# wo of kv head 0 by eight 8-partition transfers, two more wo parts in mid-stream, last product and result in two rows: one decode block on one core

## Chip, cores and metric

One core of one Trainium2 chip. The metric is the device time of the whole program in microseconds, lower is better. Within one set of rounds the executions of the kernel before spread over 0.4 to 0.9 us, so most runs were timed in five rounds, in turn with the kernel before on the same chip. The sets ran on different chips: e1 to e4 on chip 10, e5 to e8 and e13 to e18 on chip 6, e9 to e12 on chip 14. For e13 to e16, eleven of the twelve executions of the kernel before are those of e5 to e8.

## The reference, cut to what matters

One token goes through an adaLN-conditioned block: attention over a cache of 32,768 positions with 32 query heads on 8 kv heads, its output projection `wo`, and a ReLU feed-forward part.

```python
h = _layernorm(x) * (1 + ca) + sa
q = (h @ wq)                                  # 32 heads of 128
scores = einsum(q, k) * Dh ** -0.5            # k_cache: (1, 8, 32768, 128) bf16, 67 MB
o = einsum(softmax(scores), v)                # v_cache: the same size
x = x + ga * (o.reshape(1, 1, 4096) @ wo)     # wo: (4096, 512) bf16, 4.2 MB
h = _layernorm(x) * (1 + cb) + sb
x = x + gb * (relu(h @ w1) @ w2)              # w1: (512, 1792), w2: (1792, 512)
return x                                      # (1, 1, 512) bf16
```

Nearly all of it is reading 149.4 MB once.

## The kernel before

All large loads go out from one queue (SP) in a fixed order, `stream`, into a ring of four slots of 32 KB per partition. A load can go out when the tile four places ahead of it in the stream has been consumed. A K or V tile is 4 MB and fills a slot; a wo part takes a whole slot too, however small.

```python
WOP = [(0, Hkv // 2), (Hkv // 2, Hkv // 4), (3 * Hkv // 4, Hkv // 4)]   # wo parts: heads 0-3, 4-5, 6-7
ring = ctx.enter_context(tc.tile_pool(name="ring", bufs=4))
...
stream = [("wm",), ("wq",)] + [("k", 0, (2 * G, 2 * G + 1)) for G in range(NG)]
for g in range(LAST):
    for G in range(NG):
        stream += [(kind, gg, (2 * G, 2 * G + 1)) for kind, gg in (("k", g + 1), ("v", g))]
stream += [("v", LAST, (0, 1)), ("v", LAST, (2,)), ("wo", 0), ("wo", 1), ("v", LAST, (3,)), ("wo", 2)]
stream += [("w1",)] + [("w2", i) for i in range(len(W2P))]
...
# the tail: x1 in four rows (partitions 0, 32, 64, 96), then for each w2 part
for i in range(KT):                                   # KT = 4
    nc.tensor.matmul(
        ffn_ps[32 * i:32 * i + 1, :], lhsT=hidT[:, ft:ft + 1],
        rhs=w2_sb[:, a, b, i * P:(i + 1) * P], start=False, stop=(ft == FT - 1), ...)
...
nc.vector.tensor_tensor(out=o_rows[:], in0=ffn_ps, in1=gb_rows[:], op=ALU.mult)
nc.vector.tensor_tensor(out=o_bf[:], in0=o_rows[:], in1=x1_rows[:], op=ALU.add)
nc.scalar.dma_start(out=out[0, 0].rearrange("(i n) -> i n", i=KT), in_=o_bf[...][:, 0, :])   # 4 rows of 256 B
```

## Time and profile before

| | before |
|---|---|
| median of all runs of the first comparison | 357.46 us (357.26 to 357.66, 4 runs) |
| span of the profiled run | 355.8 us |
| bytes read | 149.43 MB, 432 GB/s over the middle 300 us |
| last V part consumed from | 340.22 us |
| first product with w2 from | 349.56 us |
| last DVE operation ends, span ends | 353.06 us, 355.8 us |

The share of busy time says little here: the DMA share is full from the first slice to the last, so the table follows the tail.

### The profile page before, as it was taken

Reading aid. Unit: us, or ns where it says so; the run is one execution under the profiler, and the core shown is the slowest. Engines: PE = TensorE matmul, PEld = TensorE weight load, DVE = VectorE, ACT = ScalarE, POOL = GpSimd, SP = SyncE. Lnnn points to the kernel's source line nnn. Section 1 sums busy time; section 2 is a strip of 40 time slices with the busy share of each in tenths; the row PEclk is TensorE's granted clock in tenths of the full one; section 3 lists DMA queues with packets and bytes.
Section 4 is the critical chain, followed back from the end, with each engine's and each line's share of the span. In section 5 each row is a group of like instructions: output and inputs, shape, how many; then the busy total and the mean of one; then the engine's idle time right before and its main releaser. Section 6 shows DMA issues by size and latency. Waiting matters only on the chain.

```text
span 355.8 us, 4200 instructions
## 1 busy us (share of the span) xinstructions
PE 274.2 (77%) x1859; PEld 129.9 (37%) x1859; DVE 188.0 (53%) x210; ACT 30.8 (9%) x74; POOL 8.5 (2%) x14
## 2 busy tenths in 40 slices
PE   0552875998689885998499849987799859987754
PEld 0540322343333342443244324433243324335753
DVE  8414696783297409661759157642937184832020
ACT  1022002201200120001100120012000110003000
POOL 9000000000000000000000000000000000000000
PEclk9999968799969996999699978998599969997555
DMA  8999999999999999999999999999999999999993
GB/s 321 442 422 440 431 427 442 429 425 438 435 426 438 431 422 446 427 431 440 424 442 435 422 443 427 431 437 427 431 437 428 427 438 433 424 437 424 408 411 130
DMA packets 6604, 149.69 MB, mean 421 GB/s; under 512 B 697, under 2 KB 698, under 8 KB 1594
## 3 DMA queue, kind: packets, MB, share of 16 engines
q1 hardware_dynamic: 6578, 149.43, 97.9%
q8 instruction: 14, 0.23, 0.2%
q14 instruction: 4, 0.03, 0.0%
q10 hardware_dynamic: 8, 0.00, 0.0%
HBM read 149.42 MB, written 0.00 MB: 420 GB/s over the span
## 4 chain that ended last, share of the span: by engine, by line
DMA 47%; PE 34%; DVE 14%; issue 3%; ACT 0%; SPq 0%; DVEq 0%
DMA Ksb<-in_A_k_cache_dram 42%; PE S_ps L343 18%; PE o_ps L412 12%; DVE KTt L334 11%; DMA Vsb<-in_A_v_cache_dram 3%; DMA w_sb<-in_B_w_dram 2%; PE oT_ps L402 1%; DVE PT_g L381 1%; PE oT_ps L429 1%; DVE S_g L349 1%; PE L_ps L386 0%; SPq L118 0%; PE attnT_ps L461 0%; PE mT_ps L359 0%; ACT X L426 0%
## 5 line engine op out<-in xcount | busy, mean ns | idle before, releaser
L343 PE MATMUL S_ps<-KTt,qbd 128*128 128x512 bf16 x512 | 134.5, 423 | 29.8 <-DVE KTt L334 29.7
L334 DVE STREAM_TRANSPOSE KTt<-Ksb 128x2048 f32<-128x2048 f32 x64 | 142.6, 2279 | 21.1 <-DMA Ksb<-in_A_k_cache_dram 17.0
L412 PE MATMUL o_ps<-Vsb,PT_g 128*16 128x512 bf16 x448 | 99.0, 379 | 0.0
L343 PEld LDWEIGHTS <-qbd 128*128 128x128 bf16 x512 | 53.8, 106 | 104.6 <-issue 53.8
L412 PEld LDWEIGHTS <-PT_g 128*16 128x16 bf16 x448 | 39.1, 90 | 56.8 <-issue 3.0
L436 DVE TENSOR_TENSOR oT_sb<-oT_ps,Linv 128x4 bf16<-128x4 f32 x8 | 1.3, 162 | 71.8 <-PE oT_ps L429 57.3
L349 DVE TENSOR_SCALAR_CACHE_REDUCE S_g<-S_ps 128x512 f32<-128x512 f32 x16 | 11.1, 691 | 41.3 <-PE S_ps L343 41.3
L314 ACT COPY qbd<-qrep_sb 32x128 bf16<-32x128 bf16 x32 | 9.4, 295 | 160.0 <-PE S_ps L343 158.9
L386 PE MATMUL L_ps<-Lexp,ones_f 128*128 128x4 f32 x16 | 3.9, 314 | 13.0 <-DVE Lexp L384 13.0
L426 ACT COPY X<-o_ps 16x512 f32<-16x512 f32 x7 | 4.0, 574 | 110.4 <-PE o_ps L412 110.4
L402 PE MATMUL oT_ps<-PT_g,Vsb 128*128 128x4 bf16 x256 | 7.3, 166 | 4.4 <-DMA Vsb<-in_A_v_cache_dram 2.8
L381 DVE STREAM_TRANSPOSE PT_g<-P_g 128x1024 bf16<-128x1024 bf16 x8 | 9.9, 1232 | 0.0
L429 PE MATMUL oT_ps<-osel,X 16*128 16x4 f32 x56 | 7.3, 250 | 2.5 <-ACT nbias L373 2.5
L197 PE MATMUL xc_ps<-one,c_bd 8*128 8x1 bf16 x4 | 0.3, 172 | 11.6 <-DVE c_bd L187 11.6
L376 ACT ACTIVATE P_g<-S_g,nbias 128x1024 bf16<-128x1024 f32 x8 | 9.2, 1147 | 0.2
L402 PEld LDWEIGHTS <-Vsb 128*128 128x128 bf16 x256 | 7.2, 105 | 4.5 <-DMA Vsb<-in_A_v_cache_dram 2.9
L359 PE MATMUL mT_ps<-ident_f,m_p 128*1 128x128 f32 x8 | 2.2, 269 | 8.4 <-DVE m_p L357 8.4
L386 PEld LDWEIGHTS L_ps<-Lexp,ones_f 128*128 128x128 f32 x16 | 3.6, 271 | 13.5 <-issue 13.4
L155 DVE COPY sel<-ident_bf 128x128 bf16<-128x128 bf16 x4 | 7.8, 3823 | 0.4 <-POOL ident_bf masks.py:199 0.4
L429 PEld LDWEIGHTS oT_ps<-osel,X 16*128 16x128 f32 x56 | 6.7, 186 | 3.1 <-ACT nbias L373 3.1
L292 PE MATMUL qT_ps<-hT,wq_sb 128*128 128x1 bf16 x128 | 3.6, 165 | 3.2 <-DMA wq_sb<-in_A_wq_dram 3.2
L359 PEld LDWEIGHTS mT_ps<-ident_f,m_p 128*1 128x1 f32 x8 | 0.6, 80 | 12.2 <-issue 9.2
(94 smaller groups left out, 79.4 us busy)
## 6 DMA issues: line engine op xcount, KB each, us to landing
Ksb<-in_A_k_cache_dram SPq DMA_DIRECT2D x16, 4096.0 KB, 29.7
Vsb<-in_A_v_cache_dram SPq DMA_DIRECT2D x15, 4096.0 KB, 25.5
wq_sb<-in_A_wq_dram SPq DMA_DIRECT2D x1, 4096.0 KB, 19.7
Vsb<-in_A_v_cache_dram SPq DMA_DIRECT2D x2, 2048.0 KB, 15.5
wm_sb<-in_w_mod_dram SPq DMA_DIRECT2D x1, 3072.0 KB, 10.2
wo_sb<-in_A_wo_dram SPq DMA_DIRECT2D x1, 2048.0 KB
wo_sb<-in_A_wo_dram SPq DMA_DIRECT2D x2, 1024.0 KB, 10.2
w_sb<-in_B_w_dram SPq DMA_DIRECT2D x1, 1792.0 KB, 10.5
```

The source lines that it names most:

```text
L155: nc.vector.tensor_copy(out=sel[:, hp, :].rearrange("p (a c) -> p a c", a=4), in_=src)
L314: nc.scalar.copy(out=o, in_=i)
L334: nc.vector.transpose(out=KTt[:].bitcast(F32), in_=Ksb[:, 32 * half:32 * half + 32, :].rearrange("p j d -> p (j d)").bitcast(F32),)
L343: nc.tensor.matmul(S_ps[:], lhsT=qbd[g % 2][:, hp, s, :], rhs=KTv[:, 16 * sl:16 * sl + 16, h, :, par], start=(t4 == 0 and sl == 0 and hp = ...
L349: nc.vector.tensor_scalar(out=S_tiles[g][:, G, :], in0=S_ps[:], scalar1=1.0, scalar2=None, op0=ALU.mult, op1=ALU.max, accum_out=m_tiles[g] ...
L376: nc.scalar.activation(out=P_g[:], in_=S_g[:].rearrange("p g f -> p (g f)"), func=ACT.Exp, bias=nbias[:], scale=scale, accum_out=l_g[:],)
L381: nc.vector.transpose(out=PT_g[:], in_=P_g[:])
L386: nc.tensor.matmul(L_ps[:], lhsT=ones_f[:], rhs=Lexp[:], start=True, stop=True)
L402: nc.tensor.matmul(o_tiles[g][:], lhsT=Vsb[:, j, :], rhs=PT_g[:, c0:c0 + REP], start=(u == 0 and j == 0), stop=(u == NTILE - 1 and j == TK ...
L412: nc.tensor.matmul(o_tiles[g][:], lhsT=PT_g[:, c0:c0 + 16], rhs=Vsb.rearrange("p (s j) d -> p s j d", j=16)[:, :, j, :], start=(u == 0 and ...
L426: nc.scalar.copy(out=X[:], in_=oT_ps[:])
L429: nc.tensor.matmul(oT_ps[:], lhsT=X[:, s * Dh:(s + 1) * Dh], rhs=osel[:, s, :], start=(s == 0), stop=(s == 3),)
```

## The change

The intent: take wo out of the tail, load the DMA engines more evenly at its end, and make the last product with fewer and wider matmuls and full 512 B rows of output. Cut to its core:

```diff
-    WOP = [(0, Hkv // 2), (Hkv // 2, Hkv // 4), (3 * Hkv // 4, Hkv // 4)]
+    WOP = [(0, 1, P // 2), (1, 1, P), (2, 2, P), (4, 2, P), (6, 2, P)]     # first head, heads, partitions
+    NROW = 2
+    RW = D // NROW
@@ load
+        if kind == "wo_lo":
+            lo = 32 * (key[1] // 4) + key[1] % 4
+            stream_dma(wo_lo[lo:lo + 29:4], wo_v(0)[lo:lo + 29:4])      # 8 partitions of 8 KB
@@ stream
     for g in range(LAST):
+        if g == Hkv // 2:
+            stream += [("wo", 1), ("wo", 2)]
         for G in range(NG):
-            stream += [(kind, gg, (2 * G, 2 * G + 1)) for kind, gg in (("k", g + 1), ("v", g))]
-    stream += [("v", LAST, (0, 1)), ("v", LAST, (2,)), ("wo", 0), ("wo", 1), ("v", LAST, (3,)), ("wo", 2)]
+            for kind, gg in (("k", g + 1), ("v", g)):
+                stream.append((kind, gg, (2 * G, 2 * G + 1)))
+                if 1 <= g < 3:
+                    stream.append(("wo_lo", 4 * (g - 1) + 2 * G + (kind == "v")))
+    stream += [("v", LAST, (0, 1)), ("v", LAST, (2,)), ("wo", 3), ("v", LAST, (3,)), ("wo", 4)]
@@ main loop
+        if g == Hkv // 2:
+            for i in range(3):
+                project(i)
@@ tail
-                for i in range(KT):
+                for i in range(NROW):
                     nc.tensor.matmul(
                         ffn_ps[32 * i:32 * i + 1, :], lhsT=hidT[:, ft:ft + 1],
-                        rhs=w2_sb[:, a, b, i * P:(i + 1) * P], ...
+                        rhs=w2_sb[:, a, b, i * RW:(i + 1) * RW], ...
-    nc.scalar.dma_start(out=out[0, 0].rearrange("(i n) -> i n", i=KT), in_=...)
+    nc.sync.dma_start(out=out[0, :, 0:RW], in_=o_bf[0:1, :])
+    nc.scalar.dma_start(out=out[0, :, RW:2 * RW], in_=o_bf[32:33, :])
```

(Cut: the same row change for x1 and gb, two fewer buffers in a pool, and the bookkeeping of parts with a partition count.)

## The prediction

> **What bounds the kernel now.** I read the page first, for the DMA strip and the issue sizes; then windows over the stream and the last microseconds; then the chain that ended last; then the timeline of the tail, for durations.
>
> The page's strip shows a core whose transfers never pause: after the first slice the DMA share is full until the last one.
>
> ```profile
> DMA  8999999999999999999999999999999999999993
> GB/s 321 442 422 440 431 427 442 429 425 438 435 426 438 431 422 446 427 431 440 424 442 435 422 443 427 431 437 427 431 437 428 427 438 433 424 437 424 408 411 130
> q1 hardware_dynamic: 6578, 149.43, 97.9%
> ```
>
> The windows give the rate: 432 GB/s at a share of 1.00 over 300 us. 149.43 MB at that rate is 346 us, so bytes are the floor and no engine's arithmetic can shorten the middle. Columns: window, its length, busy time of PE, PEld, DVE, ACT and POOL, granted clock, DMA share, GB/s.
>
> ```profile
> 20.00:320.00 300.00, 246.60 (x1164) 105.82 (x1165) 171.34 (x160) 24.12 (x63) 0.00 (x0) 0.90 1.00 432
> 320.00:348.00 28.00, 19.61 (x486) 16.97 (x485) 3.86 (x19) 3.72 (x7) 0.00 (x0) 0.60 0.99 414
> ```
>
> Quarter microseconds at the end show how the stream runs out.
>
> ```profile
> 348.50:348.75 0.25, 0.09 (x4) 0.00 (x1) 0.00 (x0) 0.13 (x1) 0.00 (x0) 0.50 1.07 410
> 348.75:349.00 0.25, 0.00 (x0) 0.08 (x1) 0.00 (x0) 0.06 (x1) 0.00 (x0) 0.50 0.86 328
> 349.00:349.25 0.25, 0.00 (x0) 0.00 (x0) 0.00 (x0) 0.00 (x0) 0.00 (x0) 0.50 0.64 246
> ...
> 349.75:350.00 0.25, 0.25 (x20) 0.25 (x16) 0.00 (x0) 0.00 (x0) 0.00 (x0) 0.50 0.55 188
> 350.00:350.25 0.25, 0.25 (x20) 0.25 (x12) 0.00 (x0) 0.00 (x0) 0.00 (x0) 0.50 0.32 123
> ...
> 350.75:351.00 0.25, 0.15 (x8) 0.15 (x11) 0.00 (x0) 0.00 (x0) 0.00 (x0) 0.50 0.17 49
> 351.00:351.25 0.25, 0.25 (x16) 0.25 (x9) 0.00 (x0) 0.00 (x0) 0.00 (x0) 0.50 0.08 16
> ```
>
> The share falls from 1.07 to about 0.55 within half a microsecond, stays there, and only then trickles out until 351.3. About eight of the sixteen DMA engines are done at 349.0; the others end between 350.0 and 351.3, on average some 1.8 us later. The profile names no DMA engine, so which eight are late is not seen.
>
> The end of the chain (start us, us, what) shows what follows:
>
> ```profile
> 330.82 9.35 DMA Vsb<-in_A_v_cache_dram
> ...
> 344.27 7.63 DMA w_sb<-in_B_w_dram
> 351.90 0.04 issue
> 351.94 0.41 PE ffn_ps L525 x7
> 352.35 0.02 issue
> 352.38 0.30 DVE o_rows L531
> 352.68 0.03 issue
> 352.71 0.02 DVEq L533
> 352.73 0.04 issue
> 352.77 0.29 DVE o_bf L533
> ```
>
> The last piece of w2 lands at 351.90 and releases the last product, two DVE operations and the store, which takes the remaining 2.7 us to 355.8. hidT was ready at 348.80 and even the first w2 piece was waited for. So the path is: slowest DMA engine, product, DVE, store.
>
> **What the Trainium skill says.** "DMA: Bandwidth & Descriptors", section "Why a DMA increments its semaphore by 16 and not by 1": a transfer uses the largest k up to 16 engines that divides the slowest dimension, on this queue the lowest-numbered k. So an 8-partition transfer runs on engines 0 to 7 only. The same page, "The descriptor swizzle": in a 128-partition transfer each engine serves 8 partitions, engines 0 to 7 partitions 0 to 63. This trace has no view by engine; the drop to half of the engines at 349.0 is compatible with two groups of eight. The same page, "Specifications": below 512 B the engines do read-modify-write. The output is now four rows of 256 B, and will be two of 512 B; this trace does not separate that cost. "TensorEngine Tiling (Array Packing)", "Key Properties": different tiles can work in parallel. The trace agrees: L525 takes 1.02, 0.60 and 0.38 us for 32, 16 and 8 matmuls, so 0.026 us each and 0.18 us latency. One 512-column S_ps matmul takes 0.219 us at full clock (7.00 us for 32), so 128 columns at the tail's clock of 0.50 would take 0.109 us alone. Hence four run side by side.
>
> **The change part by part.**
>
> 1. *wo of head 0 by engines 0 to 7.* 64 partitions of 8 KB = 512 KB. Shared evenly it is 32 KB per engine; now engines 0 to 7 carry 64 KB each and the others none. At 432/16 = 27 GB/s, 32 KB is 1.2 us: engines 0 to 7 end 1.2 us later, the others 1.2 us earlier. If the late ones are 8 to 15, 349.0 becomes about 350.2 and 351.3 about 350.1: nearly level. The shape of the change (why else avoid 16 engines) makes me believe this. I take 1.0 us for all landings late in the stream. The added issues, eight of about 0.36 us on SP, lie in gaps between issues of over 3 us: no cost.
>
> 2. *Two more wo parts in mid-stream.* No bytes are removed. Each takes a whole one of the four ring slots for only 0.5 and 1 MB (1.2 and 2.4 us). Usually a K transfer takes 29.7 us from issue to landing, 9.7 of them its own, so up to 20 us of work is queued ahead. Behind the small parts less is: with the K tile before them landing at T, V ends at T+9.7 and the parts at T+13.3. The next K is issued when that K tile's four transposes (9.0 us) are done, so 4.3 us before the queue empties; the next V when the older V is consumed at about T+19.8 (in the trace, a K landing at 186.7 and that issue at 206.47), against a queue that lasts to T+23: 3.2 us. Positive both times, so I charge nothing. The projections (32+16+32 matmuls at 0.037 us, 3 us) move into the stream where PE is not the bound. V and K of the last head land about 4.9 us later (2.1 MB moved ahead of them), but PV of the third V quarter and the projection still finish before the last V part at about 340: no cost.
>
> 3. *Last product in two rows.* Matmuls of 256 columns, two side by side: 0.219/2 = 0.109 us each. Parts of 16, 8 and 4 take 1.75, 0.88 and 0.44 us plus 0.18 latency. With landings 1.0 us earlier: the first part starts at 348.55, ends at 350.3; the second 351.2; the third is then held by PE, not by its landing at 350.9, and ends at 351.8 including latency. Before it was 352.35. So of 1.0 us won, 0.55 survives.
>
> 4. *Two DVE operations on 64x256 instead of 128x128.* The 128-element ones take 0.29 us, the 4-element ones 0.16, so one element costs 0.00104 us: 0.43 us each, +0.27 us.
>
> 5. *Store.* One issue on ACT of 1.10 us with four rows becomes one row on ACT and one on SP (x_row's single-row issue took 0.23 us on SP, other SP issues 0.33 to 0.39). ACT's issue still comes last. For fewer rows and 512 B writes I allow 0.3 us, an estimate without a row behind it.
>
> x1_rows and gb_rows get fewer, wider matmuls and a copy 0.1 us longer, beside the layernorm and long before they are used: nothing.
>
> Sum: -0.55 + 0.27 - 0.30 = -0.6 us, so 357.34 becomes about 356.7.
>
> **The rivals.** (a) *The late engines are not 8 to 15*, or are spread over both halves. Then the slowest engine gets 1.2 us more, the last part is bound by its landing again, and its product takes 0.62 instead of 0.38 us: +1.2 + 0.24 + 0.27 - 0.3 = +1.4, 358.7. For it: no view by engine. Against it: the abrupt fall to half. (b) *The ring starves in mid-stream.* Slack of 3 to 4 us assumes that all sixteen engines stand at the same place; the early eight are ahead, and issue to first byte costs something (the first bytes move about 0.8 us after the first issue at 0.74). Were 1 to 2 us lost twice, part would remain as a hole in the stream: 357.5 to 359. (c) *The balance gains nothing at the end* because the early engines' lead is made only by the last small transfers: then only the tail counts, +0.24 + 0.27 - 0.3: 357.5. (d) *Everything won arrives at the end*: the products keep up with the landings and the store is quicker: 355.8.
>
> **Range and chances.** The central path has perhaps 60%, (c) and (d) each about 12%, (a) and (b) together 16%. That gives 356.7 with 355.7 to 358.0 for 8 in 10. A 2% change is 7.1 us; the bytes forbid gaining it, and no wait found here could lose it. Faster 0.01, same 0.98, slower 0.01.
>
> **What would show it.** Right: in quarter-microsecond windows at the end the DMA share falls from full to near zero within about 1 us, without a plateau at one half; the last w2 landing comes near 350.9; the last V part lands near 339.2; the share stays at 1.00 around the two mid-stream parts; L548 takes about 1.9, 1.05 and 0.62 us for 16, 8 and 4, the last two without a wait for the DMA; o_rows and o_bf take 0.43 us. Wrong: a longer plateau (rival a), a dip below 0.9 after the two parts or an SP wait for attnT_ps in mid-stream (rival b), a store longer than 2.7 us.

## The result, and the profile after

The changed kernel took 358.47 us (median of 4, 358.13 to 359.42) against 357.46 (4 runs): 1.0033 of before, 95% interval 1.0012 to 1.0053. A ratio is the mean time of one kernel's runs over that of the other's runs of the same rounds, so it is not quite the ratio of the medians quoted. Ten executions over two occasions have a mean of 358.6 and lie between 357.65 and 359.42. The predicted range ended at 358.0.

The end of the chain that ended last, of the changed kernel (start us, us, what):

```profile
338.54 11.44 DMA w_sb<-in_B_w_dram
...
350.02 3.17 PE ffn_ps L548 x28
...
353.21 0.43 DVE o_rows L554
...
353.73 0.42 DVE o_bf L556
```

All 28 matmuls of the product are on the path now, in one unbroken piece that starts at the first w2 piece; in the profile of the kernel before only the last 7 were. The DVE operations take 0.42 us instead of 0.29. The store takes 356.4 - 354.15 = 2.25 us instead of 355.8 - 353.06 = 2.74.

But most of the time was not lost here. PE's timeline, first of the kernel before, then of the changed one (start us, us, instruction, in brackets the idle time before it and what ended it):

```profile
340.22 1.87 PE L402 MATMUL oT_ps<-PT_g,Vsb 128*128 128x4 bf16 x64 [2.82 <-DMA Vsb<-in_A_v_cache_dram]
...
349.56 1.02 PE L525 MATMUL ffn_ps<-w_sb,hidT 128*1 128x128 bf16 x32 [0.98 <-DMA w_sb<-in_B_w_dram]
```

```profile
340.88 1.86 PE L423 MATMUL oT_ps<-PT_g,Vsb 128*128 128x4 bf16 x64 [2.37 <-DMA Vsb<-in_A_v_cache_dram]
...
350.02 3.15 PE L548 MATMUL ffn_ps<-w_sb,hidT 128*1 128x256 bf16 x28 [0.80 <-DMA w_sb<-in_B_w_dram]
```

The work on the last V part starts 0.66 us later, after the same number of bytes. From there to the end of the span it is 355.8 - 340.22 = 15.58 us before and 356.4 - 340.88 = 15.52 us after, which looks as if the two-row tail gave back what it takes. The other profiles say that it does not. This profile of the kernel before is the only one of a four-row kernel in which the last piece of the product comes apart from the one before it; in e8_split, which has the same product, the last two pieces run as one:

```profile
349.74 1.02 PE L525 MATMUL ffn_ps<-w_sb,hidT 128*1 128x128 bf16 x32 [0.80 <-DMA w_sb<-in_B_w_dram]
351.01 1.01 PE L525 MATMUL ffn_ps<-w_sb,hidT 128*1 128x128 bf16 x24 [0.26 <-DMA w_sb<-in_B_w_dram]
```

There the product ends 11.43 us after the start on the last V part, in the other three four-row kernels (e1, e10, e17) after 11.54 to 11.85, in the profile above after 12.10. From the last V part to the end of the span those four take 15.00 to 15.23 us. Eleven profiles of two-row kernels (all but four, e4, e7, e9 and e13, in which hidT, the row that the product reads, had to wait for w1) take 15.42 to 15.76 us. So the two-row tail costs some 0.4 us.

The rest of the loss is in the stream. Windows over 180 to 240 us (PE, PEld, DVE, ACT, POOL busy, then clock, DMA share, GB/s), before and then after:

```profile
180.00:240.00 60.00, 52.93 (x238) 22.41 (x237) 34.42 (x33) 4.23 (x12) 0.00 (x0) 0.94 1.00 432
```

```profile
180.00:240.00 60.00, 49.93 (x255) 21.72 (x254) 31.24 (x28) 3.06 (x8) 0.00 (x0) 0.91 1.00 424
```

8 GB/s over 60 us is 0.48 MB, or 1.1 us of transfer, missing just where the two mid-stream parts go by. Elsewhere the two kernels move the same bytes in the same time (within 0.1 us of transfer up to 180 us). The same stretch runs at 421 to 425 GB/s in all five profiles with the two slots (the changed kernel, e1, e9, e12, e18) and at 429 to 434 in all others but that of e15, which has three slots. Note the share: 1.00 in both. It counts the time that packets take, and packets that take longer fill it as well as bytes do; only GB/s showed the loss.

At the end of the stream, in quarter microseconds, the plateau at one half is gone, as predicted. But a shelf at 0.7 stands in its place until 350.75, and the engines end later, not earlier:

```profile
350.00:350.25 0.25, 0.23 (x4) 0.15 (x5) 0.00 (x0) 0.00 (x0) 0.00 (x0) 0.50 0.74 287
...
350.50:350.75 0.25, 0.25 (x6) 0.17 (x4) 0.00 (x0) 0.00 (x0) 0.00 (x0) 0.50 0.71 246
...
351.25:351.50 0.25, 0.25 (x7) 0.17 (x4) 0.00 (x0) 0.00 (x0) 0.00 (x0) 0.50 0.09 33
```

The last bytes move at about 351.4 before and 351.6 now. More engines are still at work late than before, so the level was reached by losing, not by winning.

### The profile page after: what moved, and what is told of

Its sections match the earlier page's. It is cut to its first block, busy times and chain, and to the rows that moved or that the text cites. A ratio compares the mean times of both kernels' runs of the same rounds, so it can differ in the third digit from the quotient of the medians.

```text
span 356.4 us, 4129 instructions
## 1 busy us (share of the span) xinstructions
PE 275.6 (77%) x1817; PEld 130.4 (37%) x1817; DVE 189.5 (53%) x212; ACT 31.2 (9%) x74; POOL 8.5 (2%) x14
## 3 DMA queue, kind: packets, MB, share of 16 engines
q1 hardware_dynamic: 6852, 149.43, 98.0%
## 4 chain that ended last, share of the span: by engine, by line
DMA 52%; PE 26%; DVE 16%; issue 4%; SPq 0%; ACT 0%; DVEq 0%
DMA Ksb<-in_A_k_cache_dram 49%; DVE KTt L355 14%; PE S_ps L364 12%; PE o_ps L433 10%; DMA w_sb<-in_B_w_dram 3%; PE oT_ps L423 1%; PE ffn_ps L548 1%; DVE S_g L370 1%; DVE PT_g L402 1%; PE oT_ps L450 1%; PE attnT_ps L482 0%; SPq L133 0%; PE mT_ps L380 0%; PE L_ps L407 0%; PE Mb_ps L392 0%
## 5 line engine op out<-in xcount | busy, mean ns | idle before, releaser
L364 PEld LDWEIGHTS <-qbd 128*128 128x128 bf16 x512 | 52.9, 105 | 109.9 <-issue 59.2
L409 DVE RECIPROCAL Linv<-L_ps 128x4 f32<-128x4 f32 x8 | 1.5, 183 | 12.7 <-PE L_ps L407 11.5
L407 PEld LDWEIGHTS L_ps<-Lexp,ones_f 128*128 128x128 f32 x16 | 2.8, 213 | 10.7 <-issue 10.5
```

The costliest lines, as they stand in the source:

```text
L364: nc.tensor.matmul(S_ps[:], lhsT=qbd[g % 2][:, hp, s, :], rhs=KTv[:, 16 * sl:16 * sl + 16, h, :, par], start=(t4 == 0 and sl == 0 and hp = ...
L407: nc.tensor.matmul(L_ps[:], lhsT=ones_f[:], rhs=Lexp[:], start=True, stop=True)
```

## The experiments

Eighteen runs were made; all gave right results.

### The tail alone, and the change without it

e1_rows4: the changed kernel with four rows and the old store.

```diff
-    NROW = 2
+    NROW = 4
-    nc.sync.dma_start(...); nc.scalar.dma_start(...)
+    nc.scalar.dma_start(out=out[0, 0].rearrange("(i n) -> i n", i=NROW), in_=...)
```

> The changed kernel with its last product, x1 rows and store put back to four rows of 128, its wo traffic kept. Theory (two costs: a last product that PE cannot finish in time, and a hole in the stream behind the two small mid-stream parts): the tail costs +0.84 (product 3.19 instead of about 2.4 us behind its first landing), +0.27 (DVE), -0.5 (store), so about 0.6 us are won back: some 0.4 us above the kernel before. Rival (all of the loss is in the stream): it stays at +1.0 us. Rival (the tail is all of it): level with before or faster.

Measured: 359.00 us, 1.0047 of before (1.0034 to 1.0059). The time did not fall, so the expectation of +0.4 us is refuted. That all of the loss is in the stream is not shown by it: in this profile the tail takes 15.23 us, 0.3 less than the changed kernel's, but the last V part was consumed from 341.97, 1.75 us later than before and 1.1 later than in the changed kernel's profile. The spread of the stream hid what the tail won.

e2_rows2: the kernel before with the two-row product and store.

```diff
-    for i in range(KT):   # four rows of 128
+    for i in range(NROW): # two rows of 256, NROW = 2, and the store in two single rows
```

> The kernel before with the two-row product and store alone, wo traffic untouched. Theory: the first w2 piece lands at 349.56 as before, 28 matmuls of 0.109 us end at about 352.7 instead of 352.35, DVE +0.27, store -0.5: between 0 and +0.3 us against before. Rival (the tail is all of the loss): +1.0 us.

Measured: 357.74 us, 1.0015 (1.0001 to 1.0029), so +0.5 us by the means and +0.3 by the medians; from the last V part to the end 355.8 - 340.24 = 15.56 us. The interval runs from 0.04 to 1.0 us, so this run alone does not bound the share of the tail; it agrees with the 0.4 us of the profiles above.

e8_split: the kernel before with four rows, only the store cut in two.

```diff
-    nc.scalar.dma_start(out=o_v, in_=r_v)          # 4 rows
+    nc.sync.dma_start(out=o_v[0:2], in_=r_v[0:2])
+    nc.scalar.dma_start(out=o_v[2:4], in_=r_v[2:4])
```

> The kernel before with its four-row product, only the store cut into two transfers of two rows, one on SP and one on ACT. Theory (of the two-row tail only the store is a gain, 0.5 us, and the product and DVE operations lose it): 0.3 to 0.5 us faster than before. Rival (the gain is from single rows of 512 B, not from two issuers): within 0.1 us of before.

Measured: 357.52 us, 1.0004 (0.9992 to 1.0016): no gain. From the end of the last DVE operation (352.77) to the end of the span it took 2.93 us, against 2.74 for one four-row transfer and 2.25 for two single rows of 512 B. The gain in the changed kernel's store is not from having two issuers. ACT's issue instruction took 1.34 us here, 1.10 with four rows and 0.50 with a single row, so the form of the transfer is what matters; whether the width of 512 B has a part in it was not separated.

### Which part of the wo traffic

e3_nomid: heads 1 to 3 of wo back in the tail, in one slot with heads 4 and 5; the eight transfers stay.

```diff
-        if g == Hkv // 2:
-            stream += [("wo", 1), ("wo", 2)]
-    stream += [..., ("v", LAST, (2,)), ("wo", 3), ("v", LAST, (3,)), ("wo", 4)]
+    stream += [..., ("v", LAST, (2,)), ("wo123",), ("v", LAST, (3,)), ("wo", 4)]   # 20 rows in one slot
```

> The changed kernel with wo of heads 1 to 3 taken out of mid-stream and put, in one ring slot with heads 4 and 5, into the tail; head 0 still by eight 8-partition transfers, two rows kept. Theory (the two small ring slots leave a hole of about 0.9 us at 208 to 212 us): 0.7 to 1.0 us faster than the changed kernel, no dip of the DMA share there. Rival (the loss is not in the ring, the dip is made up later): within 0.2 us of the changed kernel.

Measured: 358.86 us, 1.0039 (1.0027 to 1.0052). The hole was gone (432 GB/s in every stage of the stream), but not the loss: the last V part came at 341.47, and two of the sixteen engines' worth of share (0.13 to 0.15) went on until 352. At this point the theory of the hole looked wrong.

e4_k16: head 0 by four transfers of 16 partitions.

```diff
-            lo = 32 * (key[1] // 4) + key[1] % 4
-            stream_dma(wo_lo[lo:lo + 29:4], wo_v(0)[lo:lo + 29:4])
+            lo = 8 * key[1]
+            if key[1] % 2 == 0:
+                stream_dma(wo_lo[lo:lo + 16], wo_v(0)[lo:lo + 16])
```

> The changed kernel with wo of head 0 by four transfers of 16 partitions, so that all sixteen engines share it: the balancing is undone, nothing else. Theory (the balancing works but is hidden by the other two costs): 0.4 to 1.0 us slower than the changed kernel and a plateau of the DMA share at about one half at the end, of over 1 us. Rival (engines 0 to 7 are the late ones, or the balance does not matter): equal or faster.

Measured: 363.44 us, 1.0165 (1.0151 to 1.0179), 5 us slower than the changed kernel. This was not the clean undo that it was meant to be. Windows of 2 us around one such transfer (issued at 67.51, queued behind two tiles):

```profile
86.00:88.00 2.00, 2.00 (x11) 0.81 (x9) 0.00 (x0) 0.00 (x0) 0.00 (x0) 1.00 1.44 487
88.00:90.00 2.00, 2.00 (x11) 0.83 (x10) 0.00 (x0) 0.00 (x0) 0.00 (x0) 1.00 1.04 315
90.00:92.00 2.00, 1.75 (x9) 0.73 (x7) 0.00 (x0) 0.52 (x2) 0.00 (x0) 1.00 0.66 279
```

A share above 1 cannot be busy time; a window seems to book the whole time of a packet where the packet starts (208.0 to 208.5 us of e15 has a share of 3.70). 1.44 with 487 GB/s and then 1.04 with 315, where elsewhere 1.00 goes with 432, are packets that take longer than their bytes do. The Trainium skill offers a reason, "SBUF — State Buffer", section "Door 1: The DMA port swizzle": four neighbouring partitions share a port, so 16 neighbours reach only 4 of the 16 ports. An estimate from that and the 27 GB/s per engine: 128 KB over four ports is 1.2 us, so 4.9 us for the four transfers. The same bytes would take 1.2 us in all over sixteen engines, so 3.7 us are lost if everything else stands meanwhile. Measured are 5.0 us over the changed kernel, and 60 to 180 us of this stream are 2.1 MB short, or 4.9 us. The trace agrees with the size, not closely; no run separates the ports from another cause. By the same map the changed kernel's step of four partitions avoids this.

e5_even: as e3_nomid, but head 0 by one ordinary 128-partition transfer.

```diff
-    WOP = [(0, 1, P // 2), (1, 1, P), ...
+    WOP = [(0, 1, P), (1, 1, P), ...
-            stream_dma(wo_lo[lo:lo + 29:4], wo_v(0)[lo:lo + 29:4])     # eight times
+            stream_dma(wo_lo[:], wo_v(0))                              # once
```

> As the run without mid-stream parts (two rows kept), but wo of head 0 comes by one ordinary 128-partition transfer of 4 KB per partition at the place of the last of the eight: every engine carries the same 32 KB. Theory (the eight transfers give engines 0 to 7 32 KB more than the others, 1.2 us at 27 GB/s, and those engines are the ones that everything waits for): about 1.1 us faster than the run without mid-stream parts, so level with the two-row run, +0.2 to +0.5 us against before; last V part lands near 340.2. Rival (the eight transfers cost nothing, the loss is in the moved order): stays at +1.4 us.

Measured: 357.68 us, 1.0008 (0.9995 to 1.0021), the last V part at 340.42. With even loading the loss was gone.

e6_sixteen: as e3_nomid, each of the eight transfers in two halves.

```diff
-            stream_dma(wo_lo[lo:lo + 29:4], wo_v(0)[lo:lo + 29:4])
+            for r in (0, 4):
+                stream_dma(wo_lo[lo:lo + 29:4, r:r + 4], wo_v(0)[lo:lo + 29:4, r:r + 4])
```

> As the run without mid-stream parts, but each of the eight transfers is cut into two of 4 KB per partition: the same bytes on the same engines, twice as many transfers. Theory (bytes on engines 0 to 7): unchanged, +1.4 us against before. Rival (each small transfer disturbs the stream by a fixed 0.15 us): another 1.2 us, +2.6 us.

Measured: 1.0016 (1.0000 to 1.0032); but its six executions were 357.35, 357.62, 357.80, 357.87 and 359.06, 359.19: two groups. Neither the fixed cost per transfer (+2.6) nor the bytes alone (+1.4 every time) fit.

e7_double: as e3_nomid, heads 0 and 1 by sixteen 8-partition transfers, the second eight on partitions 64 to 127.

```diff
-            stream_dma(wo_lo[lo:lo + 29:4], wo_v(0)[lo:lo + 29:4])
+            for h in (0, P // 2):
+                stream_dma(wo_lo[h + lo:h + lo + 29:4], wo_v(0)[h + lo:h + lo + 29:4])
```

> As the run without mid-stream parts, but heads 0 and 1 on 128 partitions by sixteen 8-partition transfers of 8 KB: twice the bytes on engines 0 to 7. Theory (bytes): another 1.2 us, +2.6 us against before, and a longer plateau of the DMA share at one half at the end. Rival (engines 0 to 7 were early and the first 512 KB nearly balanced them): the same +2.6 or less. Rival (count of transfers): as the run with sixteen half transfers.

Measured: 362.0 us, 1.0122 (1.0109 to 1.0135): +4.4, more than the +2.6 expected. The stream itself lost rate (421 GB/s instead of 433 over 60 to 140 us), which the bytes theory did not foresee. Engines 0 to 7 may meet the other engines at the ports of the upper half; that is argued, not shown, and this run says little about the dose.

### Probes: where the engines stand

Tiny transfers of 1, 2, 4, 8 and 16 partitions were queued right behind the last V part and read by GpSimd, in three kernels. By "DMA: Bandwidth & Descriptors", "Why a DMA increments its semaphore by 16 and not by 1", they run on engine 0, 0 to 1, 0 to 3, 0 to 7 and all. The count of packets agrees with that rule: the changed kernel has 6,852 on the main queue against 6,578, and the difference of 274 comes out exactly with 8 data and 8 completion packets for each of the eight transfers (128), 144 for one more 128-partition transfer and 2 for the row of the result that SP now stores. The kernel before with probes has 110 more, two for each partition of its seven probes. Which engines these are no trace shows.

```diff
+            for k in (1, 2, 4, 8, 16):
+                t = const.tile([k, 16], BF16)
+                stream_dma(t[:], A_wo[0:k, 0:16])
+                nc.gpsimd.tensor_copy(out=pr_out[0:k, :], in_=t[:])
```

> The kernel before with tiny probe transfers of 1, 2, 4, 8 and 16 partitions of 32 B queued right behind the last V part, read by the idle GpSimd in that order: the read of the 8-partition probe starts when engines 0 to 7 have got that far, the 16-partition one when all have. Two more (8, 16) in mid-stream. Theory A (engines 0 to 7 are the late ones already in the kernel before): the 8-partition probe lands with the last V part, the 16-partition one at the same time. Theory B (engines 8 to 15 are late, as the prediction had it): the 8-partition probe lands 1 us or more before the 16-partition one. Time within 0.5 us of before.

> The same probes in the run without mid-stream parts (eight transfers kept). Theory (the 32 KB make engines of 0 to 7 the last): the 8-partition probe lands with the last V part, 1 us later than in the kernel before, and the 16-partition one at the same time. If the 1- to 4-partition probes land clearly earlier, a few of engines 4 to 7 are the late ones, not all eight. Rival (other engines are the last): the 8-partition probe lands well before the 16-partition one.

> The same probes in the changed kernel. Theory (the mid-stream hole levels the engines at the price of bytes not moved): all probes land within some 0.6 us of each other, at about the landing of the last V part. Rival: the 8-partition probe lands well before the 16-partition one.

GpSimd's timeline in the kernel before with probes; each start is the time when the engines up to that number had got through the last V part (reads are in order, and the first row holds two):

```profile
338.13 0.43 POOL L128 COPY pr_out<-pr_end 1x16 bf16<-1x16 bf16 x2 [180.20 <-DMA pr_end<-in_A_wo_dram]
339.08 0.19 POOL L128 COPY pr_out<-pr_end 4x16 bf16<-4x16 bf16 x1 [0.52 <-DMA pr_end<-in_A_wo_dram]
340.29 0.19 POOL L128 COPY pr_out<-pr_end 8x16 bf16<-8x16 bf16 x1 [1.03 <-DMA pr_end<-in_A_wo_dram]
340.80 0.19 POOL L128 COPY pr_out<-pr_end 16x16 bf16<-16x16 bf16 x1 [0.32 <-DMA pr_end<-in_A_wo_dram]
```

Engines 0 and 1 are 2.5 us ahead of the last one, 2 and 3 are done by 339.08, but the slowest of 4 to 7 stands only 0.5 us before the slowest of 8 to 15. The picture behind the prediction, in which the early eight are engines 0 to 7, is wrong here; Theory A and Theory B of the expectation are both wrong in their plain form. Another 1.2 us for all of 0 to 7 would put the slowest of 4 to 7 at 341.5 and make it the last. In the changed kernel:

```profile
338.96 0.19 POOL L143 COPY pr_out<-pr_end 1x16 bf16<-1x16 bf16 x1 [179.23 <-DMA pr_end<-in_A_wo_dram]
...
340.47 0.19 POOL L143 COPY pr_out<-pr_end 4x16 bf16<-4x16 bf16 x1 [0.93 <-DMA pr_end<-in_A_wo_dram]
342.08 0.44 POOL L143 COPY pr_out<-pr_end 8x16 bf16<-8x16 bf16 x2 [1.42 <-DMA pr_end<-in_A_wo_dram]
```

The 8-partition probe is the last to land; the 16-partition one was there when it was read. In this execution one of engines 4 to 7 closes the V part, 1.6 us after engines 0 to 3. The expected levelling to within 0.6 us is not there. Times: e10 357.5 us, 1.0003 (the probes cost nothing there); e12 359.61 us, 1.0066 (1.0052 to 1.0079), which is 1.1 us more than the changed kernel without probes. And e11, the run without mid-stream parts with probes, took 357.54 us, 1.0005, 357.49 to 357.65 in all four executions, with all probes down by 340.6: the 1.4 us that this kernel had lost without probes, on another chip, were not there. So the probes, or the chip, may have changed what they were to measure in e11 and e12. One profile each: these are single pictures of engines, not averages.

### The mid-stream parts, by themselves, by cure and by dose

e9_mid_even: all of the change but the eight transfers (head 0 by one 128-partition transfer, as in e5_even).

> The changed kernel with its mid-stream parts and two rows, but wo of head 0 by one ordinary 128-partition transfer: all of the change except the eight small transfers. Theory (only the eight transfers hurt; the mid-stream hole starves engines that are ahead and would wait anyway): within 0.5 us of before, about 357.8. Rival (the mid-stream hole costs its 0.9 us by itself): about 358.6.

Measured: 358.66 us, 1.0029 (1.0015 to 1.0043), executions 358.12 to 359.81. The rival was right: with even loading the kernel with mid-stream parts takes 0.9 us more than e5_even by the means (0.75 by the ratios). The profile of e9 is of the slowest execution, 359.81, with a wait of 1.35 us for w1 in the tail that no other profile has (0.49 at most); its stream is read here, not its tail.

e13_oneslot: the changed kernel with its two mid-stream parts in one slot. e14_oneslot_even: the same with even head 0.

```diff
-            stream += [("wo", 1), ("wo", 2)]
+            stream += [("wo12",)]
+        if kind == "wo12":
+            t = ring.tile([P, 12, D], BF16, tag="slot", name="wo_sb")   # both parts, still two transfers
```

> The changed kernel with its two mid-stream parts in one ring slot instead of two, still two transfers and all else kept, the eight small transfers too. Theory 1 (two small slots starve the stream): the next K transfer is then issued some 7 us earlier, the K landings around the parts are 42.4 us apart (38.7 for four tiles and 3.6 for the parts) instead of 43.6, and the time falls by 0.7 to 1.2 us, to about 357.6. Theory 2 (the eight transfers are what costs): it stays at about 358.5.

> The same one slot, and wo of head 0 by one ordinary 128-partition transfer. Theory 1: 1.0 to 1.4 us faster than the run with mid-stream parts and even head 0 (+1.4 us), so about +0.3 us against before, and level with the one-slot run that keeps the eight transfers. Theory 2: level with before as well, but 0.7 to 1.2 us faster than the one-slot run that keeps the eight transfers.

Measured: e14 357.85 us, 1.0006 (0.9993 to 1.0019), so the cure works: 0.8 us better than e9. Its window over 180 to 240 us is back at the rate of before, where e9 had 425; e9 first, then e14:

```profile
180.00:240.00 60.00, 51.42 (x253) 22.11 (x252) 31.39 (x28) 3.06 (x8) 0.00 (x0) 0.86 1.00 425
```

```profile
180.00:240.00 60.00, 51.73 (x270) 22.86 (x269) 32.64 (x28) 3.06 (x8) 0.00 (x0) 0.94 1.00 432
```

Why it works is seen in SP's timeline of the changed kernel and then of e13 (start us, us, what was issued):

```profile
180.47 9.43 SPq L133 DMA_DIRECT2D wo_sb<-in_A_wo_dram  x2
196.92 0.33 SPq L133 DMA_DIRECT2D Ksb<-in_A_k_cache_dram  x1
207.12 0.33 SPq L133 DMA_DIRECT2D Vsb<-in_A_v_cache_dram  x1
```

```profile
180.25 0.80 SPq L141 DMA_DIRECT2D wo_sb<-in_A_wo_dram  x2
189.50 0.33 SPq L141 DMA_DIRECT2D Ksb<-in_A_k_cache_dram  x1
196.69 0.33 SPq L141 DMA_DIRECT2D Vsb<-in_A_v_cache_dram  x1
```

With one slot the K and V behind the parts go out 7.4 and 10.4 us earlier. But e13 took 359.08 us, 1.0043 (1.0030 to 1.0056): one execution of 357.69 (the profiled one, with the expected fast stream) and four of 359.03 to 359.12. So Theory 2 has its share too, in most executions of this build: with the eight transfers kept, the one slot won nothing by the means (358.8 against 358.6 us).

e15_threeslots: the same 1.5 MB in three slots.

```diff
-    WOP = [..., (1, 1, P), (2, 2, P), ...]
-            stream += [("wo", 1), ("wo", 2)]
+    WOP = [..., (1, 1, P), (2, 1, P), (3, 1, P), ...]
+            stream += [("wo", 1), ("wo", 2), ("wo", 3)]
```

> The changed kernel with the same 1.5 MB of mid-stream wo cut into three ring slots (heads 1, 2 and 3). Theory 1, by dose: the next K must now wait until the V tile before the parts is consumed, 19.2 us after the landing of the K tile before it, while the queue is empty after 13.3 us: a stop of 6 to 7.5 us that the end sees in full, about 365. Theory 2 (the slots do not matter): 358.5.

Measured: 366.93 us, 1.0262 (1.0247 to 1.0276): 8.5 us over the changed kernel, somewhat more than expected. Windows of 2 us:

```profile
198.00:200.00 2.00, 1.02 (x6) 0.28 (x5) 0.85 (x3) 1.15 (x4) 0.00 (x0) 1.00 0.84 334
200.00:202.00 2.00, 2.00 (x11) 0.87 (x11) 0.49 (x2) 0.03 (x1) 0.00 (x0) 1.00 0.09 35
202.00:204.00 2.00, 2.00 (x11) 0.81 (x9) 0.00 (x0) 0.00 (x0) 0.00 (x0) 1.00 0.00 0
...
208.00:210.00 2.00, 1.48 (x24) 1.38 (x21) 0.45 (x3) 1.04 (x2) 0.00 (x0) 1.00 1.15 360
```

The stream stands still from about 201.2 to 208: the next K was issued at 207.06 and its first packets are at 208.0. Two more things are to be seen. The queue does not end at once but tails off from 199.5 to 201.2, engine by engine; and after the restart the first 2 us carry 360 GB/s at a share of 1.15, the same low rate at a full share that the changed kernel shows at 208 to 210 us (360 at 1.05).

### Repetitions and the remainder

e16_nomid_again: e3_nomid unaltered. e17_one_even_rows4: e14 with four rows and the old store. e18_after_again: the changed kernel unaltered.

> The run without mid-stream parts again, unaltered, on another occasion. Theory 2 (the eight transfers cost 1.2 us every time): +1.4 us against before again. If the loss belonged to that one occasion: +0.3 us, like the run with even head 0 and the one with probes.

> One slot for the mid-stream parts, even head 0, and the last product and store back in four rows: 2 MB of wo are still moved forward, all three suspected costs are gone. If they are all there is: within 0.2 us of before. If the moved order has a cost of its own: 0.5 us or more above before.

> The changed kernel itself again, unaltered, on the same chip: between 358.0 and 359.5, +0.8 to +1.4 us against before; no execution below 357.9, since the hole of two slots is there in every one of them.

Measured: e16 357.75 us, 1.0009 (0.9994 to 1.0024), executions 357.26, 357.50, 357.75, 357.82 and 359.06: the kernel that had lost 1.4 us in five of five on chip 10 now lost it in one of five on chip 6. The chip alone does not decide it: e13 lost it in four of five on chip 6. Over all kernels with the eight transfers and without the two slots (e3, e6, e11, e13, e16), 25 executions, 13 lie between 357.26 and 357.87 and 12 between 358.71 and 359.19, none between. The kernels with even loading and without the two slots (e5, e14, e17), 14 executions, have none above 358.26. In the slow profile of e16 the K landings stand 0.1 us behind those of the fast profile of e13 at 70.5 us, 1.0 at 109, and 1.1 at 149, which looks like a lag that grows while the eight transfers pass (66 to 131 us). But e3's slow profile is 0.8 us behind e13's at the first K already, and still 0.8 at 149; and against e11's fast profile, the same stream with probes, the lag of e16 is 1.2 us at 188 and 0.3 at 305. Where a slow execution loses its time stays open.

e17: 357.65 us, 0.9996 (0.9984 to 1.0008): with all three costs gone and 2 MB of wo still moved forward, nothing is left. Against e14, which differs from it in the rows alone, it is 0.4 us less by the ratios; that is within the intervals and in keeping with the 0.4 us of the tails. e18: 358.83 us, 1.0025 (1.0009 to 1.0042), executions from 357.65 to 359.32; that none would be below 357.9 was wrong. No version came out clearly faster than the kernel before.

## Why the prediction was wrong, point by point

What bounds the kernel (bytes, then the tail) held, and so did "no 2% either way". The time missed the range by 0.5 us. The sum had -0.6 us, and +1.0 came out (by the medians): two steps failed in the same direction, where the sum had no cost for either, and the product, which was to bring 0.55 us, brought none.

**Step 1, "If the late ones are 8 to 15 ... I take 1.0 us for all landings late in the stream", failed.** The last V part came at 340.9 instead of 339.2. The share at the end shows how many engines work, not which. The probes showed engines 0 to 3 ahead and the slowest of 4 to 7 nearly as late as that of 8 to 15, so the eight transfers can make one of 4 to 7 the last, as it is in e12's profile. The gain of 1.0 us is in no execution: the fastest with the eight transfers, 357.26 (e16), is level with the kernel before. Their cost is 0 in some executions and about 1.3 us in others, and even loading removes the slower group: that much is shown. That 32 KB is 1.2 us is in keeping with it; the way from the 32 KB to the loss is argued. Why an execution falls into one group or the other is not settled. Rival (a), with 358.7, had named this step; that the measured time lies so near is partly luck, since (a) holds only one of the losses.

**Step 2, "Positive both times, so I charge nothing", failed.** The issue times were right to 0.6 us (with T at 187.9 they came at 196.92 for T+9.0 = 196.9 and at 207.12 for T+19.8 = 207.7), yet 0.48 MB went missing. Shown by cure and dose: one slot instead of two wins 0.8 us, three instead of two cost 8.5. What the slack of 3.2 us left out: engines up to 2.7 us apart at one place in the stream (the probes), about 1 us from issue to the first packet and a slow first 2 us (e15). That these three use it up is arithmetic from different runs; which engines ran dry in the changed kernel was not seen. Rival (b) had named it, with 357.5 to 359, and got too small a weight. Its signs would not have told: the dip of the DMA share (0.76 at 210 to 212 us) and the SP wait for attnT_ps in mid-stream (4.3 us) are there, but e14, which has lost nothing, has 0.80 and 5.5 us.

**Step 3, the product, had the right durations and the wrong start.** 28 matmuls took 3.15 us, 0.112 each (0.109 predicted). But their start does not seem to follow a w2 landing: from the start on the last V part to the first product it is 9.14 us in the changed kernel, 9.15 in e2 and 9.15 in e3, and at most 9.29 in the eleven two-row profiles without a wait for w1. The two-row tail is a chain behind the last V part. The chain's word that a w2 landing released the product misled; PE waits about as long (0.77 to 0.94 us) in every two-row profile. And the 352.35 that the product was to beat came from the odd profile: in the other four-row kernels the product ends 11.4 to 11.9 us after the start on the last V part, with two rows after 12.3 us. Instead of 0.55 us won, some 0.4 to 0.9 were lost against these.

**Step 4** held: 0.42 us each, +0.26. **Step 5**, the estimate without a row behind it, was short: 0.5 us instead of 0.3.

The losses do not add: the hole (+0.8), the eight transfers (0 or +1.3) and the tail (some +0.4: the product, the DVE operations and the store together) came to +1.2 and +0.9 by the two ratios of the changed kernel. The reason may be that the V part waits for one slowest engine and that each loss of the stream falls on some engines only; that is argued.

## What to carry to other kernels

In a stream through a ring of slots, a small tile costs a whole slot: count what is left queued when the slot's user is finally consumed, and ask for several microseconds of it, not for "positive". Pack small loads together in one slot. Do not balance DMA engines by a share curve: probe with transfers of 1, 2, 4 and 8 partitions first, and repeat executions, since a loss of 1.3 us that came five times of five was gone in four of five on another occasion and chip. Do not read a tail from one profile: the one of the kernel before hid 0.4 us.

## What the Trainium skill lacked or had wrong

- "DMA: Bandwidth & Descriptors": the page gives a first-byte latency of about 0.6 us, but not that a queue has to hold several microseconds of work per engine to keep all sixteen moving. Here 3 to 4 us, by the prediction's count of what is queued, cost 0.8 us, 7 us more of it cost nothing, and after a full stop the first packets came 0.95 us after the issue, with 360 instead of 432 GB/s over the next 2 us.
- The same page, "Latency and other measured facts", has engines 7 and 15 as usually the slower ones, with a best guess that ties this to transfers issued by GpSimd, which this kernel does not use. No run here singles out one engine, but in one profile engines 0 and 1 were 2.5 us, and 2 and 3 at least 1.7 us, ahead of the last one after 340 us of even load.
- The same page's "Use all 16 engines" says that a transfer of fewer partitions is confined to fewer engines, not that executions with such transfers can fall into two groups: 357.3 to 357.9 and 358.7 to 359.2 us here, and no second group without them (the kernels with two slots apart).
- "SBUF — State Buffer", section "Door 1: The DMA port swizzle": it agreed in size (16 neighbouring partitions, 5.0 us for four transfers of 128 KB), but the section does not say what such a transfer does to the rest of the stream: at each of the four a window of 2 us is down to 279 to 311 GB/s.
- No page has the issue time of a small store on ACT by its form: 1.10 us with four rows of 256 B, 1.34 with two (two more going out on SP), 0.50 with one of 512 B (one more on SP).
